# An attention and softplus-MLP kernel: the scheduler's order and pools replaced by one written list of steps and places, and GpSimd's copies and subtractions given to the other engines

## The chip, the cores and the metric

One NeuronCore of a Trainium2 chip. The metric is the device time of one execution in microseconds (us). TensorE is PE in the profile, VectorE DVE, ScalarE ACT, GpSimd POOL, and SyncE (which issues all DMAs here) SP.

## The reference

```python
B, H, S, Ns, D = 8, 8, 512, 32, 64          # x: (B, H, S, D), state: (B, H, Ns, D)
a      = softmax(x @ state^T / 8)           # over the 32 states
xread  = a @ state                          # (B, H, 512, 64)
a2     = softmax(state @ x^T / 8)           # over the 512 positions
sread  = a2 @ x                             # (B, H, 32, 64)
X = concat(xread, sread) -> (B * 544, 512)  # heads side by side
h = X @ w_in                                # 512 -> 2048
out = softplus(h) @ w_out                   # 2048 -> 512, (4352, 512) in float32
```

`w_in` and `w_out` arrive as float64 and are turned into float32 on the chip, by integer operations on their halves.

## The kernel before

**What is computed how.** The 512 rows `xread` of a batch are never formed. Since `xread @ w_in = a @ (state @ w_in)`, the kernel first forms V = state x w_in for every batch, and the hidden layer is then the attention weights times V. The 32 rows `sread` of each batch are formed and multiplied with w_in at the end for all batches together ("the read rows"). To keep float32's accuracy at the speed of fp32r, nearly every operand is split into a high part in fp32r (a copy that rounds) and a low part (the difference), and a product is three matmuls: high x high, high x low, low x high. A split is one copy and one subtraction of a 128x512 tile:

```python
def split(hi, lo, src, *what):
    if ("hi",) + what in MOVED:
        pool_copy(hi, src)                                  # GpSimd, L98
    else:
        nc.scalar.copy(hi, src)                             # ACT, L105
    vec(*what).tensor_tensor(lo, src, f32(hi), ALU.subtract)  # L106, DVE, or GpSimd where MOVED says so
```

Lines that matter in the profile:

- L112 loads a float64 tile. L129 or L136 (ACT; L134 on GpSimd) scales its high word, L131 (DVE, one instruction) or the pair L140, L141 (DVE, on 16-bit halves) shapes the low word, L142 (DVE) joins them.
- L185 and L194 (first chunk of 512 columns, two halves of 256), L227 and L238 (the other three chunks): plain float32 products of w_in with the state, for batches 0 and 1, and for 2 and 3. L190 to L199, L232 to L243 copy them out of PSUM. The converted weights and the products for batches 2 and 3 go out to DRAM.
- L262: the products for batches 4 to 7, by reading the weights back and splitting them (L276 or L98, L277) and copying the result out (L265, L267), in the stretch from about 200 us on.
- L322 loads x transposed, 512 KB at once. L369: scores of batches 0 and 1 in plain float32; L375: of the others in fp32r, whose two halves L379 and L380 add. L383 to L401: softmax over the states (transpose, maximum, difference, exponential, sum, product, transpose back); L406 to L415 over the positions. L425 transposes (TensorE), L443 and L449 read x, L455 to L469 scale, L477 and L486 transpose to `sreadT`.
- L513: the hidden layer of one of 16 tiles of 128 units ("h", six matmuls of 512 columns). L500: softplus. L520: the output layer, twelve matmuls of one tile for four chunks of 128 rows, into four accumulators "acc". L560: hidden layer of the read rows. L609 and L612: partial sums of batches 0 and 1. L160 and L162 copy the accumulators out, L528 stores them.

**What sets the order.** The program is written as strings of letters (START, BLOCK, LAST and others), each letter one piece of work: a hidden tile, an output tile, a split, a load, a step of the softmax. A scheduler then places the instructions on the engines' queues. The tile turns are: batch 0, tiles 0 to 3; batch 1, tiles 0 to 7; batch 0, 4 to 11; batch 1, 8 to 15; batch 0, 12 to 15; then batches 2 to 6, then the read rows, then batch 7. The weights of w_in and w_out are converted along the way. Buffers come from pools by tags with one to four buffers each; of PSUM's eight banks two belong to "aux" (scores, products, transposes), two to h and four to acc. The set MOVED names copies and subtractions that go to GpSimd.

Of the kernel before, what the change touches and what calls it, by code (L numbers as in the profile page):

```python
# [49 lines left out]
def attention_then_softplus_mlp(ctx: ExitStack, tc, xn, xt, zq, zp, stk, w_in, w_out, out):  # L50
    nc = tc.nc
    nc.scalar.preload_act_table_set("natural_log_exp_and_others")

    cp = ctx.enter_context(tc.tile_pool(name="cp", bufs=1))
    sp = ctx.enter_context(tc.tile_pool(name="sp", bufs=1))
    dp = ctx.enter_context(tc.tile_pool(name="dp", bufs=1, space=DRAM))
    ps = ctx.enter_context(tc.tile_pool(name="ps", bufs=1, space=PSUM))
    uid = [0]

    def sb(tag, shape, dt=F32, bufs=1):  # L60
        uid[0] += 1
        return sp.tile(shape, dt, tag=tag, name=f"{tag}_{uid[0]}", bufs=bufs)

    def bank(tag, bufs):
        uid[0] += 1
        return ps.tile([P, 512], F32, tag=tag, name=f"{tag}_{uid[0]}", bufs=bufs)

    BANKS = {"aux": 2, "h": 2, "acc": 4}
    turn = cycle(("h", "acc", "acc"))
    early = [True]  # L70

    def aux():
        if early[0]:
            tag = next(turn)
            return bank(tag, BANKS[tag])
        return bank("aux", 2)

    ident = cp.tile([P, P], F32, name="ident")
    make_identity(nc, ident)


    if WARM:
        idle = sb("sr", [P, P], bufs=2)
        nc.vector.memset(idle, 0.0)
        pb = aux()
        for _ in range(WARM):
            nc.tensor.matmul(pb[:, 0:P], idle, idle, start=True, stop=True)

    def rouse():
        pb = aux()  # L90
        for c in range(4):
            nc.tensor.transpose(pb[:, P * c:P * c + P], ident, ident)

    def vec(*what):
        return nc.gpsimd if what in MOVED else nc.vector

    def pool_copy(dst, src):
        nc.gpsimd.tensor_scalar(dst, src, 1.0, 0.0, ALU.mult, ALU.add)  # L98


    def split(hi, lo, src, *what):
        if ("hi",) + what in MOVED:
            pool_copy(hi, src)
        else:
            nc.scalar.copy(hi, src)  # L105
        vec(*what).tensor_tensor(lo, src, f32(hi), ALU.subtract)  # L106

    def load_w(src, tag=None):
        w64 = src.dtype == I64
        tag = tag or ("k4" if w64 else "wt")  # L110
        t = sb(tag, src.shape, I64 if w64 else F32, bufs=K4 if tag == "k4" else 2)
        nc.sync.dma_start(t, src)  # L112
        return t

    def as_f32(t, *what, tag="wt"):  # L120
        if t.dtype != I64:
            return t
        v = t.bitcast(I32).rearrange("p (n t) -> p n t", t=2)
        lo, hi = v[:, :, 0], v[:, :, 1]
        n = t.shape[1]
        h2 = sb("k2", [P, n], bufs=K2)
        r = sb(tag, [P, n], bufs=2 if tag == "wt" else 1)
        if early[0] or ("pre",) + what in MOVED:
            nc.scalar.activation(h2, f32(hi), AF.Prelu, scale=2.0 ** -112, alpha=-(2.0 ** 32))  # L129
            u = r.bitcast(I32)  # L130
            nc.vector.tensor_scalar(u, lo, 29, None, ALU.logical_shift_right)  # L131
        else:
            if ("h2",) + what in MOVED:
                nc.gpsimd.tensor_scalar(h2, f32(hi), 2.0 ** -112, 0.0, ALU.mult, ALU.add)  # L134
            else:
# [205 lines left out]

# [404 lines left out]
```

## Time and profile before

| | us |
|---|---|
| runs | 695.63, 697.95, 699.69 (median 697.95) |
| the profiled execution, first to last instruction | 695.4 |
| first float64 tile's conversion starts on DVE | 7.67 |
| TensorE, busy | 675.9 in 3028 matmuls |
| DVE, ACT, POOL, busy | 395.0, 390.9, 218.4 |
| moved by DMA | 82.90 MB |

The profiled execution has no other time of its own than its span, which lies at the lower end of the runs. A matmul's busy time in the profile overlaps that of the next one, so TensorE's share says that it has work nearly always and not how fast it goes through it; the starts of a string of matmuls tell that. Start times are counted from the span's start.

### The profile page before, as it was taken

How to read it: one execution, taken by the hardware profiler on the slowest of the kernel's cores; microseconds unless marked ns; L12 is line 12 of the kernel's file. 1: busy time of each engine (PE TensorE's matmuls, PEld its weight loads, DVE VectorE, ACT ScalarE, POOL GpSimd, SP SyncE). 2: the span in 40 equal slices, each digit the busy share in tenths (PEclk: the TensorE clock that was granted, in tenths of full speed). 3: DMA queues.
4: the chain of work that ended last, by engine and by line, in shares of the span. 5: the costliest groups of instructions: out<-in, count | busy, mean ns of one | idle time of the engine just before them, and what ended most of it. 6: DMA issues, size and time to landing. Idle time of an engine off the chain costs nothing.

```text
span 695.4 us, 8922 instructions
## 1 busy us (share of the span) xinstructions
PE 675.9 (97%) x3028; PEld 540.1 (78%) x3028; DVE 395.0 (57%) x692; ACT 390.9 (56%) x661; POOL 218.4 (31%) x209
## 2 busy tenths in 40 slices
PE   7879999999999999999999999999999999999997
PEld 4456667788887877888888888888888889988886
DVE  5898788319777885776556752676257423311101
ACT  4787975434848944775538634863386334423321
POOL 0130157146433584156222450235022400121310
PEclk9999999999999999999999999999999999999999
DMA  7778895103253545464423220321121113512001
GB/s 253 258 258 293 307 301 188 49 0 122 68 167 122 184 156 166 143 199 136 134 94 121 69 90 31 107 76 31 31 69 45 40 39 98 168 30 61 1 0 61
DMA packets 42061, 82.90 MB, mean 119 GB/s; under 512 B 6176, under 2 KB 13088, under 8 KB 42016
## 3 DMA queue, kind: packets, MB, share of 16 engines
q1 hardware_dynamic: 42016, 82.33, 36.1%
q8 instruction: 24, 0.39, 0.2%
q14 instruction: 21, 0.17, 0.1%
HBM read 56.62 MB, written 25.69 MB: 118 GB/s over the span
## 4 chain that ended last, share of the span: by engine, by line
PE 83%; ACT 7%; DVE 5%; DMA 2%; issue 1%; POOL 1%; SPq 0%; POOLq 0%; DVEq 0%; ACTq 0%
PE acc L520 49%; PE h L513 22%; PE h L560 3%; PE aux L262 2%; PE aux L449 2%; PE aux L375 1%; ACT L500 1%; DMA xT<-in_xt_dram 1%; ACT t L500 1%; PE aux L425 1%; PE aux L238 1%; PE aux L227 1%; DMA k<-in_w_in_dram 1%; ACT ghi L105 1%; DVE glo L106 1%
## 5 line engine op out<-in xcount | busy, mean ns | idle before, releaser
L520 PE MATMUL acc<-wout,ghi 128*128 128x512 f32 x1088 | 341.7, 395 | 3.9 <-POOL wout L98 2.8
L520 PEld LDWEIGHTS acc<-wout,ghi 128*128 128x128 f32 x1088 | 203.8, 189 | 50.7 <-issue 3.6
L520 PE MATMUL acc<-wout,glo 128*128 128x512 f32 x544 | 214.2, 394 | 0.0
L513 PE MATMUL h<-aT,vhl 128*128 128x512 f32 x768 | 199.4, 398 | 0.1
L513 PEld LDWEIGHTS h<-aT,vhl 128*128 128x128 f32 x768 | 142.1, 188 | 35.3 <-issue 3.4
L500 ACT ACTIVATE t<-h 128x512 f32<-128x512 f32 x136 | 81.0, 598 | 121.4 <-PE h L513 81.1
L106 DVE TENSOR_TENSOR glo<-t,ghi 128x512 fp32r<-128x512 f32 x83 | 63.7, 770 | 124.2 <-ACT ghi L105 83.9
L106 POOL TENSOR_TENSOR glo<-t,ghi 128x512 fp32r<-128x512 f32 x53 | 70.9, 1338 | 159.5 <-ACT ghi L105 156.7
L520 PEld LDWEIGHTS acc<-wout,glo 128*128 128x128 f32 x544 | 102.4, 188 | 23.0 <-issue 0.7
L105 ACT CAST ghi<-t 128x512 fp32r<-128x512 f32 x96 | 59.1, 618 | 76.1 <-PE acc L520 75.6
L106 DVE TENSOR_TENSOR vhl<-vf,vhl 128x512 fp32r<-128x512 f32 x57 | 41.5, 728 | 58.6 <-ACT vhl L105 48.4
L98 POOL TENSOR_SCALAR ghi<-t 128x512 fp32r<-128x512 f32 x40 | 28.7, 718 | 82.1 <-PE acc L520 39.5
L105 ACT CAST vhl<-vf 128x512 fp32r<-128x512 f32 x60 | 37.1, 618 | 17.3 <-PE h L513 11.3
L500 ACT ACT_TABLE_LOAD x23 | 29.5, 1283 | 7.8 <-DVE glo L106 5.7
L380 DVE TENSOR_TENSOR sc<-aux,k 64x512 f32<-64x512 f32 x24 | 16.4, 683 | 23.4 <-ACT k L379 23.1
L98 POOL TENSOR_SCALAR vhl<-vf 128x512 fp32r<-128x512 f32 x12 | 8.4, 696 | 66.8 <-PE h L513 50.7
L277 DVE TENSOR_TENSOR R<-wt,R 64x512 fp32r<-64x512 f32 x23 | 18.8, 819 | 10.4 <-ACT R L276 7.3
L560 PEld LDWEIGHTS h<-sreadT,vhl 128*128 128x128 f32 x192 | 24.1, 191 | 0.6
L560 PE MATMUL h<-sreadT,vhl 128*128 128x256 f32 x192 | 24.3, 283 | 0.0
L106 POOL TENSOR_TENSOR vhl<-vf,vhl 128x512 fp32r<-128x512 f32 x15 | 21.9, 1457 | 6.4 <-ACT vhl L105 6.0
L262 PE MATMUL aux<-R,StK 128*128 128x512 f32 x64 | 19.1, 398 | 1.2 <-POOL R L277 0.7
L398 POOL TENSOR_TENSOR T<-T,mx 128x512 f32<-128x512 f32 x7 | 7.7, 1106 | 37.3 <-DVE mx L397 17.4
(156 smaller groups left out, 736.3 us busy)
## 6 DMA issues: line engine op xcount, KB each, us to landing
vd<-ve SPq DMA_DIRECT2D x44, 256.0 KB, 2.7
xT<-in_xt_dram SPq DMA_DIRECT2D x16, 512.0 KB, 3.7
k<-in_w_out_dram SPq DMA_DIRECT2D x16, 512.0 KB, 5.1
x<-in_xn_dram SPq DMA_DIRECT2D x16, 512.0 KB, 3.5
vf<-vd SPq DMA_DIRECT2D x64, 128.0 KB, 2.6
k<-in_w_in_dram SPq DMA_DIRECT2D x12, 512.0 KB, 4.9
out_dram<-o SPq DMA_DIRECT2D x24, 256.0 KB, 2.2
vf<-vd SPq DMA_DIRECT2D x16, 256.0 KB, 4.0
```

What stands on the lines that cost most here:

```text
L98: nc.gpsimd.tensor_scalar(dst, src, 1.0, 0.0, ALU.mult, ALU.add)
L105: nc.scalar.copy(hi, src)
L106: vec(*what).tensor_tensor(lo, src, f32(hi), ALU.subtract)
L262: nc.tensor.matmul(pb, StK[i][:, h, :], r, start=(i == 0), stop=(i == 1))
L277: vec("R", *what, o).tensor_tensor(r[z], wf[a], f32(r[a]), ALU.subtract)
L380: nc.vector.tensor_tensor(sc[64 * j:64 * j + 64], pb[0:64], s2, ALU.add)
L398: vec("tmul", bk, g).tensor_tensor(T, T, sm.unsqueeze(2).broadcast_to([P, 16, NS]), ALU.mult)
L449: nc.tensor.matmul(pb[:, 256 * j:256 * j + 256], a2T[:, c, j].rearrange("p i n -> p (i n)"), v["xs"][j][:, c].rearrange("p i n -> p (i n)" ...
L500: nc.scalar.activation(t, h, AF.Softplus)
L513: nc.tensor.matmul(h, Vhl[b, ft // 2][:, vi, g, cs], aT[b][:, ai, g], start=(n == 0), stop=(n == 5))
L520: nc.tensor.matmul(acc[c], g[gi][:, c0:c0 + P], wout[ft][:, wi], start=(ft == first and i == 0), stop=(ft == last and i == 2))
L560: nc.tensor.matmul(h[:, 256 * i:256 * i + 256], Whl[u, i][:, wi, kt, :], sreadT[:, si, kt, :], start=(n == 0), stop=(n == 11))
```

## The change

The scheduler, the strings and MOVED go. The kernel first describes all its work as a graph of 2598 named steps with their inputs and outputs, and then walks a list, PLAN, that names each step in order, the engine that does it, and the place of every buffer that it makes: one of 69 single or 14 double places in SBUF, or one of PSUM's eight banks, which any kind of buffer may have.

```diff
-START = 'avaavaaavaavaavavavaavaaaaBpbW|bvbbbbboVbvbbbWV|bbbbVVWVaVVbVaaaaaaabbbVbap|bbbaiWgVgpVboVob|iVpbViW|gbWV|biVVibgbog|pVigW|bbVp|VoWVgi|VogpVb|ViVVpVg|
...
+PLAN = """
+Lq.1:S:0 Li.0.3:S:1 Lz.0:S:2 zn.0:G:3 Lt.0.0.0:S:4 Lt.0.0.1:S:5 Li.0.2:S:6 Li.0.7:S:7 Li.0.0:S:8 Lt.0.1.0:S:9 Lq.0:S:10 Lo.1:S:0 ch.0.3:A:11
...
+    with tc.manual_schedule():
...
+        ops = graph(io, at, nc)
+        for step in PLAN.split():
+            name, e, where = step.split(":")
+            step = ops.pop(name)
+            where = [int(w) for w in where.split(",") if w]
+            for buf in step.places():
+                if buf not in place:
+                    put(buf, where.pop(0))
+            step.emit(e)
```

The engine letters are A and C for ACT (two forms of the high half), V and W for DVE (W is the low half in two instructions), T for TensorE, S for SP, and G for GpSimd. The products, their splits and the order in which each accumulator adds up are those of before. What else is different:

- GpSimd does two clearings of a tile and the identity matrix at the start, and nothing later: its instructions go from 215 to 14. DVE's go from 695 to 784 (subtractions and the like of 128x512 from 224 to 320), ACT's from 648 to 751 (copies of 128x512 from 208 to 276; table loads from 46 to 36). TensorE's matmuls stay at 3028.
- x transposed is loaded in halves of 256 KB, and V is fetched for 256 columns at a time, so that SP issues 421 DMAs for about 325, with the same bytes.

Three places show how instructions move. In the rows the numbers behind a name are the buffer's.

The first is SP's queue at the program's start, where `xT` is x transposed, `Z`, `zf` and `QZ` the state in two layouts, `k` and `w` float64 tiles of w_in, `o` of w_out, and `x` x itself; before:

```order
L322 DMA xT_102<-in_xt_dram 128x1024
L334 DMA Z_84<-in_zp_dram 128x2x64 x2
L112 DMA k_6_104<-in_w_in_dram 128x256
L112 DMA k_7_106<-in_w_in_dram 128x256
L322 DMA xT_108<-in_xt_dram 128x1024
L112 DMA k_9_110<-in_w_in_dram 128x256
```

and now:

```order
L292 DMA QZ_103<-in_zq_dram 128x512
L292 DMA w_0_3_105<-in_w_in_dram 128x256
L292 DMA zf_107<-in_zp_dram 128x256
L292 DMA xT_0_0_111<-in_xt_dram 128x512
L292 DMA xT_0_1_113<-in_xt_dram 128x512
L292 DMA w_0_2_115<-in_w_in_dram 128x256
L292 DMA w_0_7_117<-in_w_in_dram 128x256
```

The first float64 tile has moved from the fourth of the queue's issues to the second, and x transposed from the first to the fourth, in two pieces.

The second is DVE ahead of the output layer of batch 1's tiles 4 and 5, where `glo`, now `gL`, are the low parts of the softplus, `wt`, `wf` and `ow` converted weights; before:

```order
L142 SCALAR_TENSOR_TENSOR wt_843<-k_240_842,wt_843 128x512
L140 TENSOR_SCALAR k_252_874<-k_248_868 128x512
L141 TENSOR_SCALAR k_252_874<-k_248_868 128x512
L142 SCALAR_TENSOR_TENSOR wt_872<-k_250_871,k_252_874 128x512
L106 TENSOR_TENSOR glo_790<-t_787,ghi_789 128x512
L140 TENSOR_SCALAR k_262_915<-k_217_747 128x512
L106 TENSOR_TENSOR wout_249_870<-wt_872,wout_249_870 128x512
L141 TENSOR_SCALAR k_262_915<-k_217_747 128x512
```

and now:

```order
L336 TENSOR_SCALAR ow_902<-o_10_576 128x512
L337 TENSOR_SCALAR ow_902<-o_10_576 128x512
L482 TENSOR_SCALAR rs<-rs 128x1
L483 RECIPROCAL rs<-rs 128x1
L341 SCALAR_TENSOR_TENSOR ow_902<-h_o_724,ow_902 128x512
L482 TENSOR_SCALAR rs<-rs 128x1
L483 RECIPROCAL rs<-rs 128x1
L301 TENSOR_TENSOR gL_4_928<-t_4_905,gH_4_915 128x512
L301 TENSOR_TENSOR gL_5_932<-t_5_907,gH_5_924 128x512
L527 TENSOR_SCALAR sr_939<-rp_0_735,rs 128x2x2x64
```

Both low parts of the softplus now stand on DVE, one behind the other, where DVE had one of them among the conversions and their splits and the next could go to GpSimd.

The third is TensorE at the first products for batches 4 to 7 (`aux`, now `pp`; `R` are split weights, `StK`, now `KH` and `KL`, the split state); before:

```order
L520 MATMUL acc_2124<-wout_128_451,ghi_1967 128x512
L262 MATMUL aux_2032<-R_1981,StK_1896 128x512
L262 MATMUL aux_2041<-R_1982,StK_1896 128x512
L520 MATMUL acc_2124<-wout_128_451,ghi_1967 128x512
L262 MATMUL aux_2032<-R_1981,StK_1896 128x512
L262 MATMUL aux_2041<-R_1982,StK_1896 128x512
L520 MATMUL acc_2124<-wout_128_451,glo_1968 128x512
```

and now:

```order
L304 MATMUL acc_0_2_2032<-Wl_1059,gH_9_2304 128x512
L304 MATMUL acc_0_2_2032<-Wh_1048,gL_9_2314 128x512
L304 MATMUL pp_0_0_2334<-R_0_2276,KH_0_2007 128x512
L304 MATMUL pp_0_0_2334<-R_0_2276,KL_0_2254 128x512
L304 MATMUL pp_0_4_2338<-R_4_2297,KH_1_2190 128x512
L304 MATMUL pp_0_4_2338<-R_4_2297,KL_1_2202 128x512
L304 MATMUL pp_0_1_2343<-R_1_2316,KH_0_2007 128x512
L304 MATMUL pp_0_1_2343<-R_1_2316,KL_0_2254 128x512
L304 MATMUL acc_0_1_2090<-Wh_1048,gH_9_2304 128x512
```

Two products that were woven into the output layer through the two banks of "aux" have become three, whole and one after the other, in banks 6, 7 and 4 of the eight.

More of the change, by code (lines that the diff above doesn't have):

```diff
@@ L1 @@
 from contextlib import ExitStack
-from itertools import cycle
 import concourse.bass as bass
@@ new lines, in width, with rounded @@
+def width(buf):
+    kind, *at = buf.split(".")
+    whole = at and at[0] in map(str, range(WHOLE))
+    if kind in ("vp", "pp", "qp", "gp", "rp", "tp", "h", "acc") or kind == "sc" and whole:
+        return 0
+    if kind in ("o8", "x", "xs", "Wf", "Vk"):
+        return 2
+    return 2 if kind == "w8" and at[0] != "0" or kind == "aa" and not whole else 1
+def rounded(buf):
+    kind, *at = buf.split(".")
+    return kind in ("KH", "KL", "R", "Vh", "Vl", "aH", "aL", "xh", "xl", "xs", "Wh", "Wl", "gH", "gL", "uH", "uL") \
+        or kind in ("z", "aa") and int(at[0]) >= WHOLE
@@ L89, in rouse @@
[L89 to L106, printed above, removed]
@@ L492, in split_wout @@
-    def split_wout(ft):
-        assert ft < NFT - 1 or all(made[0, c] == 3 for c in range(1, 4))
-        wout[ft] = sb(f"wout{ft}", [P, 2, DM], F32R)
-        w = as_f32(ahead("out"), ft)
-        split(wout[ft][:, 0], wout[ft][:, 1], w, "wout", ft)
-    def softplus(h, *what):
-        t = sb("t", [P, 512], bufs=2)
-        nc.scalar.activation(t, h, AF.Softplus)
-        ghi = sb("ghi", [P, 512], F32R, bufs=3)
-        glo = sb("glo", [P, 512], F32R, bufs=3)
-        split(ghi, glo, t, "g", *what)
-        return ghi, glo
@@ L506, in gemm1 @@
-    def gemm1(b, ft):
-        h = bank("h", 2)
-        n = 0
-        cs = slice(P * (ft % 2), P * (ft % 2) + P)
-        assert made["aT", b] == 2
-        for g in range(2):
-            for vi, ai in PASSES:
-                nc.tensor.matmul(h, Vhl[b, ft // 2][:, vi, g, cs], aT[b][:, ai, g], start=(n == 0), stop=(n == 5))
-                n += 1
-        return softplus(h, min(b, 4), ft)
-    def gemm2(acc, g, ft, cols, first=0, last=NFT - 1):
-        for c, c0 in enumerate(cols):
-            for i, (gi, wi) in enumerate(PASSES):
-                nc.tensor.matmul(acc[c], g[gi][:, c0:c0 + P], wout[ft][:, wi],
-                                 start=(ft == first and i == 0), stop=(ft == last and i == 2))
@@ L553, in gemm1_read @@
-    def gemm1_read(u):
-        assert made["read"] == B
-        h = bank("h", 2)
-        for i in range(2):
-            n = 0
-            for kt in range(4):
-                for wi, si in PASSES:
-                    nc.tensor.matmul(h[:, 256 * i:256 * i + 256], Whl[u, i][:, wi, kt, :], sreadT[:, si, kt, :],
-                                     start=(n == 0), stop=(n == 11))
-                    n += 1
-        return softplus(h, B, u)
-    COLS = [0, P, 2 * P, 3 * P]
-    QTR = NFT // 4
@@ L686, in attention_then_softplus_mlp @@
-    run(START)
-    assert made["read"] == 3
-    for b in range(2, B - 1):
-        run({2: BLOCK2, 3: BLOCK3}.get(b, BLOCK), b)
-    run("|gFp" * (NFT // 2))
-    run(LAST)
-    while pend:
-        flush(True)
+    io = IO()
+    io.xn, io.xt, io.zq, io.zp, io.stk, io.w_in, io.w_out, io.out = xn, xt, zq, zp, stk, w_in, w_out, out
+    io.wsc = [dp.tile([DM, 512], F32, tag=f"wsc{c}", name=f"wsc{c}") for c in range(4)]
+    io.Vd = {}
+    for c in range(4):
+        io.Vd[0, c] = dp.tile([H, P, 512] if c in PACKED else [P, 4, 512], F32, tag=f"vd0_{c}", name=f"vd0_{c}")
+        io.Vd[1, c] = dp.tile([H, P, 512], F32, tag=f"vd1_{c}", name=f"vd1_{c}")
@@ new lines, in attention_then_softplus_mlp, with put @@
+    ident = cp.tile([P, P], F32, name="ident")
+    sreadT = cp.tile([P, 2, 4, B * NS], F32R, name="sreadT")
+    fixed = {"ident": ident, "sreadT": sreadT.bitcast(F32)}
+    for n, w in SMALL.items():
+        t = cp.tile([P, 2 * B, w], F32, name=n)
+        for b in range(B):
+            for g in range(2):
+                fixed[f"{n}.{b}.{g}"] = t[:, 2 * b + g, :]
+    place = {}
+    def put(buf, i):
+        n = width(buf)
+        if n == 0:
+            place[buf] = ps.tile([P, 512], F32, tag=f"bank{i}", name=buf.replace(".", "_"), bufs=1)
+        else:
+            t = sp.tile([P, 512 * n], F32R if rounded(buf) else F32, tag=f"{'sd'[n - 1]}{i}", name=buf.replace(".", "_"), bufs=1)
+            place[buf] = t.bitcast(F32) if rounded(buf) else t
@@ new lines, in at @@
+    def at(buf):
+        return fixed[buf] if buf in fixed else place[buf]
+    with tc.manual_schedule():
+        make_identity(nc, ident)
+        put("idle", 0)
+        put("h.idle", 0)
+        nc.vector.memset(at("idle")[:, 0:P], 0.0)
+        for _ in range(WARM):
+            nc.tensor.matmul(at("h.idle")[:, 0:P], at("idle")[:, 0:P], at("idle")[:, 0:P], start=True, stop=True)
+        ops = graph(io, at, nc)
[6 more added lines that the diff above has]
+                    put(buf, where.pop(0))
+            assert not where
+            step.emit(e)
+        assert not ops
```

1081 lines of the change are left out of this document (585 added, 496 removed).

## The prediction

> **What bounds the kernel now.** I read the page first, then the chain of work that ended last, then the engines by stretches, then TensorE's groups and waits in the first stretch. The lines are the page's busy times, the end of the chain, and five stretches (length, then busy time and count for PE, PEld, DVE, ACT, POOL, then granted clock, DMA share, GB/s).
>
> ```profile
> PE 675.9 (97%) x3028; PEld 540.1 (78%) x3028; DVE 395.0 (57%) x692; ACT 390.9 (56%) x661; POOL 218.4 (31%) x209
> ...
> 675.29 16.33 PE acc L520 x72
> ...
> 0.00:90.70 90.70, 77.83 (x283) 51.56 (x284) 70.00 (x158) 69.77 (x131) 16.23 (x20) 0.98 0.79 275
> 90.70:200.00 109.30, 108.18 (x467) 85.41 (x466) 73.45 (x114) 62.42 (x102) 46.66 (x46) 1.00 0.37 120
> 200.00:300.00 100.00, 98.40 (x436) 78.43 (x436) 75.07 (x124) 64.92 (x109) 45.95 (x44) 1.00 0.50 159
> 300.00:691.20 391.20, 391.06 (x1846) 324.71 (x1845) 176.04 (x299) 193.17 (x321) 109.55 (x100) 1.00 0.23 71
> 691.20:695.40 4.20, 0.41 (x2) 0.00 (x0) 0.46 (x1) 0.58 (x1) 0.00 (x0) 1.00 0.66 247
> ```
>
> TensorE sets the end, but its 97% hides the only place with room. A record's busy time overlaps the next one's, so I count by spacing: 16.33/72 = 0.2268 us for a 512-column product in fp32r. From 300 to 691.2 TensorE runs without a gap, and the change leaves its 1846 matmuls there as they are: nothing to gain. In the first 90.7 us it starts only 283. Their groups (count, busy, mean ns, idle ahead), two strings that give the spacing in plain fp32, and its two largest waits:
>
> ```profile
> L520 PE MATMUL acc<-wout,ghi 128*128 128x512 f32 x50 | 18.4, 448 | 3.8 <-POOL wout L98 2.8 <-ACT wout L105 1.0
> L513 PE MATMUL h<-aT,vhl 128*128 128x512 f32 x60 | 17.8, 427 | 0.0
> L520 PE MATMUL acc<-wout,glo 128*128 128x512 f32 x25 | 11.5, 458 | 0.0
> L369 PE MATMUL aux<-xT,Z 128*128 128x512 f32 x16 | 8.9, 683 | 3.8 <-DMA xT<-in_xt_dram 3.6 <-DMA Z<-in_zp_dram 0.2
> L443 PE MATMUL aux<-x,a2T 128*128 128x256 f32 x32 | 7.4, 383 | 0.0
> L238 PE MATMUL aux<-wt,wout 128*128 128x512 f32 x10 | 5.3, 613 | 0.1
> ...
> L185 PE MATMUL acc<-wout,QZ 128*128 128x256 f32 x8 | 2.5, 388 | 1.2 <-DMA QZ<-in_zq_dram 1.2
> ...
> 25.86 1.98 PE L369 MATMUL aux<-xT,Z 128*128 128x512 f32 x4
> ...
> 53.81 3.48 PE aux L443 x16
> ...
> PE aux L369 <- DMA xT<-in_xt_dram: 3.6, 2, 1.9
> PE acc L520 <- POOL wout L98: 2.8, 1, 2.8
> ```
>
> Plain fp32 of 512 columns is spaced (1.98 - 0.683)/3 = 0.43, of 256 columns 3.48/16 = 0.2175. So the 283 are worth 135 x 0.2268 = 30.6 (L520, L513), 16 x 0.43 = 6.9 (L369), 28 x 0.43 = 12.0 (four groups of L227 and L238, one shown), 64 x 0.2175 = 13.9 (L443, and L185 with L194, one of seven groups shown) and 24 transposes at about a quarter of 0.43, 2.6; the rest are the warm-up, worth nothing. That is 66 us of work in 90.7: **24.7 us are lost there**, of the 41 that the span holds over all its matmuls at these spacings. DVE and ACT are occupied 70.00 and 69.77 of these 90.7 us, and their product is what TensorE waits for. The change is decided here; all else is small.
>
> **The change part by part.** First the prices: DVE's and POOL's subtraction (83 and 53 of them), ACT's and POOL's copy, a table load; then DVE's low halves of a float64 weight in two instructions (15 pairs, L140 and L141) and in one (L131), and a subtraction under POOL's.
>
> ```profile
> L106 DVE TENSOR_TENSOR glo<-t,ghi 128x512 fp32r<-128x512 f32 x83 | 63.7, 770 | 124.2 <-ACT ghi L105 83.9
> L106 POOL TENSOR_TENSOR glo<-t,ghi 128x512 fp32r<-128x512 f32 x53 | 70.9, 1338 | 159.5 <-ACT ghi L105 156.7
> ...
> L105 ACT CAST ghi<-t 128x512 fp32r<-128x512 f32 x96 | 59.1, 618 | 76.1 <-PE acc L520 75.6
> ...
> L98 POOL TENSOR_SCALAR ghi<-t 128x512 fp32r<-128x512 f32 x40 | 28.7, 718 | 82.1 <-PE acc L520 39.5
> ...
> L500 ACT ACT_TABLE_LOAD x5 | 6.4, 1283 | 0.1
> ...
> L140 DVE TENSOR_SCALAR k<-k 128x512 uint16<-128x512 uint16 x15 | 7.3, 490 | 1.0 <-DMA k<-in_w_in_dram 1.0
> L141 DVE TENSOR_SCALAR k<-k 128x512 uint16<-128x512 uint16 x15 | 7.2, 480 | 0.0
> L106 DVE TENSOR_TENSOR glo<-t,ghi 128x512 fp32r<-128x512 f32 x6 | 4.1, 686 | 0.3 <-ACT ghi L105 0.3
> L131 DVE TENSOR_SCALAR wt<-k 128x512 int32<-128x512 int32 x4 | 1.7, 423 | 1.8 <-DMA k<-in_w_out_dram 1.8
> ...
> 24.27 1.05 POOL L398 TENSOR_TENSOR T<-T,mx 128x512 f32<-128x512 f32 x1
> ...
> 24.39 1.49 DVE L106 TENSOR_TENSOR vhl<-vf,vhl 128x512 fp32r<-128x512 f32 x1
> ```
>
> A subtraction on DVE takes 0.69 alone and 1.49 while POOL subtracts. So POOL's subtractions gave DVE little: 1.34 of POOL's time, of which DVE pays up to 0.8.
>
> *DVE up to the same TensorE work (the first product of tile 5 of the second batch, matmul 283).* By its new order 31 large subtractions stand ahead, against 22 on DVE and 4 on POOL before: 9 more for DVE, +6.2. Two max-subtractions or products of the softmax come from POOL: +1.4. Low halves of 512 columns: 7 pairs and 11 single ones against 15 pairs and 4, -8 x 0.97 + 7 x 0.42 = -4.8; two of 256 columns become pairs, +0.5; one joining of halves more, +0.7. Some four evacuations at 256 or 512 columns fewer: -1.4. No slowed instructions: -1.7. Seven small subtractions of the read rows (0.22 each) come later: -1.5. Sum: -0.6, so DVE has **69.4 us to do, as before**. ACT: ten more casts, five of them POOL's, +6.2; one high half more, +0.7; three table loads fewer, -3.8; seven small casts later, -1.4; three evacuations and a scaling fewer, -2: **-0.3, 69.5 us**. POOL's 16 us are absorbed. The engines' work therefore gives no speed by itself; what may is that they idle less than 90.7 - 70 = 20.7 us.
>
> *When they start.* The first row is the first float64 load, the fourth of the old queue's issues; the second DVE's first conversion, which waited for it.
>
> ```profile
> 1.43 1.32 SPq L334 DMA_DIRECT2D Z<-in_zp_dram  x2
> 2.79 1.08 SPq L112 DMA_DIRECT2D k<-in_w_in_dram  x2
> ...
> 7.67 0.29 DVE L131 TENSOR_SCALAR wout<-k 128x256 int32<-128x256 int32 x1 [6.67 <-DMA k<-in_w_in_dram]
> ```
>
> It took 7.67 - 2.79 = 4.9 from issue to use. Now it is issued second, where the state's load was issued at 1.43: 6.3, a gain of 1.4. If all idling after that stays (90.7 - 7.67 - 70 = 13.0), matmul 283 starts at 6.3 + 69.4 + 13.0 = **88.7: the upper end**.
>
> *The lower end* is set by the DMA queue. In the new order 10.1 MB stand on it up to the weight tile with which the second chunk of columns begins on DVE (its low half), and 25.8 us of DVE's 69.4 ahead of that. At the first stretch's 275 GB/s it lands at 36.7, so at least 11 us of DVE's idling stay, and matmul 283 can't start before 36.7 + 69.4 - 25.8 + one subtraction (0.7) = **81**. Between 81 and 88.7 I take two thirds toward the upper, 86.2, since the waits that make it up (ACT's high half, transfers of w_out) are between instructions that the new order still sets close. The gain here is 90.7 - 86.2 = **4.5 us**. Two reads of the first batch now stand ahead of TensorE's first h product, and their x tiles behind some 7.9 MB, so about 29 us: covered by the 20 us that TensorE has to spare by then, but not if DVE ran ahead.
>
> *From 90.7 on.* In 200 to 300 the five largest groups hold 409 fp32r products:
>
> ```profile
> L520 PE MATMUL acc<-wout,ghi 128*128 128x512 f32 x154 | 48.4, 392 | 0.2 <-DVE StK L612 0.2
> L513 PE MATMUL h<-aT,vhl 128*128 128x512 f32 x123 | 31.5, 392 | 0.0
> L520 PE MATMUL acc<-wout,glo 128*128 128x512 f32 x78 | 30.5, 391 | 0.0
> L262 PE MATMUL aux<-R,StK 128*128 128x512 f32 x38 | 11.6, 402 | 1.2 <-POOL R L277 0.7 <-DVE sreadT L106 0.6
> L375 PE MATMUL aux<-k,zhl 128*128 128x512 f32 x16 | 4.7, 397 | 0.1
> ...
> PE aux L227 <- DVE wout L232: 1.1, 1, 1.1
> ```
>
> 92.8 us and some 3 of smaller ones: 4 lost. Of that 1.2, with 1.1 behind L232 at 97, are waits for POOL and for copies that DVE did late: **2.3 gained** if the written order has them earlier, and 0 if others come in their place. DVE gets POOL's 21 subtractions of this stretch (75.07 + 21 x 0.69 = 89.6 of 100) and ACT its 23 copies (64.92 + 23 x 0.62 = 79): covered by TensorE's 100, thinly for DVE. After 300 both have over 190 us idle, so the rest of POOL's 109.55 costs nothing. More and smaller DMAs (421 against about 325): 96 issues at about 0.54 (1.08 for two, above), 52 us on a queue that only issues; after the first 90 us nothing waits for it. The tail of 4.20 (the last products' copies and stores) keeps its form.
>
> Sum: 695.4 - 4.5 - 2.3 = 688.6 of span. The median of the runs, 697.95, stands 2.55 above the profiled span (the runs are 695.63 to 699.69, the span about the lowest): **691**.
>
> For the copies there is a rule that speaks against their move. Row: POOL's copy 718 ns, ACT's 618, and POOL's subtraction 1338 against 770. The Trainium skill, "GPSIMD Engine Reference", section 4.1, says that one-input operations run there at about line rate and only two-input ones at about half of VectorE's; the rows agree. By that rule moving the copies only loads ACT, by 7 x 0.62 = 4.3 us in the first 90 (five copies and two high halves); had ACT nothing to set against it, the time would be 695.5.
>
> **The rivals.** *No change, 697.* DVE and ACT idle as much as before (88.7, a gain of 2.0), and 90 to 300 keeps its waits: 693.4 + 2.55 = 696, and 697 with a wait of 1 us in a new place. For it: their occupied time is the same to 2 us, and a strict order stalls the whole engine at each late input.
>
> *Slower, 705.* Eight PSUM banks are now handed from buffer to buffer at once, where the score products and the packed products had two of their own. After 90 us 32 products (L262) and 24 pairs of scores (L375) each take a bank that an evacuation must have left. In 200 to 300 27 such places lost some 4 us, 0.15 each. If each of the 56 loses half an evacuation (0.3, by the copy's 0.62 above), 56 x 0.3 = 17 stand in the place of the 2.8 that the forecast leaves of them: 691 + 14 = **705**; it decides from 0.24 a place (13.2 in all, past 701.4). For it: in the written order up to three products of this kind stand back to back, and DVE is at 90% there. Against: the chain of needs, summed from the durations, leaves DVE and ACT 15 to 30 us ahead of TensorE from about 130 us on.
>
> *The clock, one step either way.* The row is five products after a gap, and the clock in the stretch behind it.
>
> ```profile
> 37.65 2.45 PE L520 MATMUL acc<-wout,ghi 128*128 128x512 f32 x5 [2.76 <-POOL wout L98]
> ...
> 38.00:39.00 1.00, 1.00 (x3) 0.76 (x3) 1.00 (x4) 1.00 (x3) 0.00 (x0) 0.50 0.31 115
> ```
>
> Half clock for about 3.4 us costs 1.7. TensorE was behind its inputs there anyhow, so it matters only past 60 us: at most 2 us, inside the range.
>
> **How the numbers follow.** A measurement of this kernel tells 0.5% (3.5 us) from no change at best: the same is 694.5 to 701.4. The forecast (faster) 0.45, no change 0.28, slower 0.27 (bank waits 0.2, other stalls 0.07). The forecast's own range is 686 (matmul 283 at 81, -9.7, and -2.3) to 694.5; for 8 in 10 the range takes in no change and most of the slower case: 685 to 705.
>
> **What would show it.** Right: matmul 283 at 81 to 89, DVE's busy time up to it near 69, no subtraction on DVE over 0.8, first conversion near 6.3; from 300 on the same distances. Wrong: waits of TensorE for an evacuation (L262's, L375's places) adding to over 5 us after 90; or DVE and ACT behind each other before 90, so that matmul 283 starts after 91; or the float64 tiles landing later than 275 GB/s gives.

## The result, and the profile after

The changed kernel takes 686.68 us (median of four runs, 686.29 to 687.10) against 697.39 before (695.63 to 699.69): ratio 0.9849, 95% interval 0.9823 to 0.9874. It is 10.7 us faster; the forecast was 691 with 685 to 705. The profiled execution took 686.29 with a span of 684.5. It moves 83.44 MB by DMA against 82.90 before, so the bytes are nearly, and not exactly, the same.

The changed kernel's page, its busy times; then the stretches (same columns as before the change), the first one ending where TensorE has done as much work as before at 90.7:

```profile
PE 668.1 (98%) x3028; PEld 541.5 (79%) x3028; DVE 403.8 (59%) x781; ACT 431.3 (63%) x764; POOL 1.6 (0%) x8
...
0.00:85.00 85.00, 74.73 (x286) 53.72 (x287) 69.53 (x154) 68.64 (x134) 1.63 (x8) 0.94 0.76 275
85.00:200.00 115.00, 115.00 (x491) 90.27 (x490) 73.88 (x138) 76.17 (x127) 0.00 (x0) 1.00 0.33 105
200.00:300.00 100.00, 97.55 (x436) 78.61 (x435) 68.29 (x120) 77.00 (x132) 0.00 (x0) 1.00 0.53 168
300.00:680.00 380.00, 379.99 (x1818) 318.59 (x1817) 192.07 (x372) 208.22 (x371) 0.00 (x0) 1.00 0.25 79
680.00:684.50 4.50, 0.81 (x4) 0.34 (x2) 0.00 (x0) 1.24 (x3) 0.00 (x0) 0.88 0.62 233
```

The first stretch holds the larger part of the gain: DVE and ACT are occupied for 69.53 and 68.64 us, as before the change (70.00, 69.77), POOL for 1.63 instead of 16.23, and the stretch is 5.7 us shorter. The two engines' work is the same and they idle less. How the engines begin, from their timelines (start, duration, idle ahead in brackets):

```profile
1.05 3.51 PE L764 MATMUL h_idle<-idle 128*128 128x128 f32 x16 [1.05 <-DVE idle L762]
...
4.59 0.39 SPq L292 DMA_DIRECT2D QZ<-in_zq_dram  x1
5.03 0.42 SPq L292 DMA_DIRECT2D w<-in_w_in_dram  x1
...
8.25 0.29 DVE L333 TENSOR_SCALAR wf<-w 128x256 int32<-128x256 int32 x1 [7.26 <-DMA w<-in_w_in_dram]
...
9.25 0.76 PE L304 MATMUL vp<-wf,QZ 128*128 128x256 f32 x1 [4.69 <-DVE wf L341]
```

And TensorE's largest waits over the whole run (sum, times, longest; `vp` is a product for V, `gp` a transpose of the exponentials `e`, `sc` the scores of the first two batches, `pp` the products for batches 4 to 7):

```profile
PE vp L304 <- DVE wf L341: 4.7, 1, 4.7
PE gp L490 <- ACT e L479: 2.4, 1, 2.4
PE sc L304 <- DMA xT<-in_xt_dram: 1.6, 1, 1.6
PE pp L304 <- DVE R L362: 1.2, 1, 1.2
PE acc L304 <- DVE gL L301: 1.1, 2, 1.0
```

The reader is to see two things. No wait is on POOL any more. And the first DMA is issued at 4.59, where it was 0.74 before: TensorE's longest wait, 4.7 us, stands behind it, and so does every other load.

Where the time went is clearest from what TensorE has lost by a given amount of work, counted by the prediction's spacings (start of the matmul that stands there, less the work ahead of it), in us. The columns on the right belong to the experiments.

| work done | before | changed | warm-up tile moved | before, no GpSimd | changed, GpSimd back | copies back | subtractions back |
|---|---|---|---|---|---|---|---|
| 15 | 13.8 | 17.3 | 12.6 | 16.9 | 17.9 | 16.8 | 18.2 |
| 66 | 24.9 | 19.0 | 14.4 | 25.2 | 22.6 | 19.5 | 21.2 |
| 180 | 27.7 | 19.6 | 15.0 | 27.3 | 25.9 | 20.2 | 22.5 |
| 300 | 32.5 | 24.6 | 20.2 | 30.1 | 34.7 | 27.5 | 29.7 |
| 650 | 36.8 | 26.0 | 21.7 | 34.4 | 36.2 | 28.9 | 31.1 |

Of the 10.8 us won, 5.9 come by 66 us of work, 2.2 up to 180, nothing between 180 and 300 (4.8 lost before, 5.0 now), 2.9 after 300 (4.3 lost before, 1.4 now).

### The profile page after: what moved, and what is told of

Read it like the earlier page. It is cut to its first block, busy times and chain, and to the rows that moved or that the text cites. A ratio compares the mean times of both kernels' runs of the same rounds, so it can differ in the third digit from the quotient of the medians.

```text
span 684.5 us, 8918 instructions
## 1 busy us (share of the span) xinstructions
PE 668.1 (98%) x3028; PEld 541.5 (79%) x3028; DVE 403.8 (59%) x781; ACT 431.3 (63%) x764; POOL 1.6 (0%) x8
## 2 busy tenths in 40 slices
DMA packets 51278, 83.44 MB, mean 122 GB/s; under 512 B 6688, under 2 KB 26144, under 8 KB 51232
## 3 DMA queue, kind: packets, MB, share of 16 engines
q1 hardware_dynamic: 51232, 82.86, 36.8%
## 4 chain that ended last, share of the span: by engine, by line
PE 85%; ACT 6%; DVE 5%; DMA 2%; issue 1%; SPq 0%; DVEq 0%; ACTq 0%
PE acc L304 49%; PE h L304 25%; PE vp L304 2%; PE rp L304 2%; PE pp L304 2%; PE qp L304 2%; DMA out_dram<-o 1%; DMA xT<-in_xt_dram 1%; PE gp L490 1%; ACT Vk L285 1%; ACT t L633 1%; PE sc L304 1%; PE h_idle L764 1%; DVE Vl L301 0%; DVE wf L341 0%
## 5 line engine op out<-in xcount | busy, mean ns | idle before, releaser
L304 PE MATMUL acc<-Wh,gH 128*128 128x512 f32 x544 | 216.7, 398 | 0.0
L304 PE MATMUL acc<-Wh,gL 128*128 128x512 f32 x544 | 212.1, 390 | 1.1 <-DVE gL L301 1.1
L304 PE MATMUL acc<-Wl,gH 128*128 128x512 f32 x544 | 212.0, 390 | 0.0
L301 DVE TENSOR_TENSOR gL<-t,gH 128x512 fp32r<-128x512 f32 x136 | 92.3, 687 | 168.5 <-ACT gH L285 163.7
L304 PEld LDWEIGHTS acc<-Wh,gL 128*128 128x128 f32 x544 | 102.1, 188 | 23.7 <-DVE gL L301 2.1
L304 PEld LDWEIGHTS acc<-Wl,gH 128*128 128x128 f32 x544 | 102.2, 188 | 22.4 <-issue 2.2
L304 PEld LDWEIGHTS acc<-Wh,gH 128*128 128x128 f32 x544 | 102.2, 188 | 22.4 <-issue 2.2
L304 PE MATMUL h<-aH,Vh 128*128 128x512 f32 x256 | 102.7, 401 | 0.5 <-ACT o L285 0.2
L304 PE MATMUL h<-aH,Vl 128*128 128x512 f32 x256 | 99.8, 390 | 0.0
L304 PE MATMUL h<-aL,Vh 128*128 128x512 f32 x256 | 99.7, 390 | 0.0
L304 PEld LDWEIGHTS h<-aL,Vh 128*128 128x128 f32 x256 | 48.1, 188 | 10.4 <-issue 1.0
L285 ACT CAST Vh<-Vf 128x512 fp32r<-128x512 f32 x48 | 29.7, 621 | 5.2 <-DMA Vf<-vd 5.2
L573 DVE TENSOR_TENSOR sc<-qp,qs 64x512 f32<-64x512 f32 x24 | 16.4, 683 | 14.9 <-ACT qs L571 14.4
```

The costliest lines, as they stand in the source:

```text
L285: nc.scalar.copy(dst, src)
L301: lambda e: eng(e).tensor_tensor(r(dlo()), src(), dhi(), ALU.subtract))
L304: nc.tensor.matmul(dst, lhs, rhs, start=start, stop=stop)
L573: lambda e, kj=kj, sc=sc, j=j: nc.vector.tensor_tensor(at(sc)[64 * j:64 * j + 64], at(f"qp.{kj}")[0:64], at(f"qs.{kj}")[0:64], ALU.add))
```

## The experiments

**The warm-up tile moved.** The row of the warm-up matmuls ends at 1.05 + 3.51 = 4.56, and the first DMA is issued at 4.59. Both have to do with place 0 of SBUF: the tile that the warm-up reads and the first load's target.

```diff
-        put("idle", 0)
+        put("idle", 68)
```

> The changed kernel, with one place moved: the tile that the eight warm-up matmuls read lies in another place of SBUF than the first load's target. In the changed kernel SP issues its first DMA at 4.59 us, just when the last warm-up matmul starts (4.46 to 4.56), where the kernel before issued at 0.74. Theory A (that load waits for the warm-up matmuls to have read their tile, and every other load stands behind it): first issue near 0.8, the first weight conversion 3.8 us earlier than 8.25, and the span shorter by 3 to 4.5 us: 682 to 684 us against 686.7, since TensorE loses 17.3 of its 26 us in the first 32. Rival B (the start is bound by how fast all the loads land, and TensorE by the work of VectorE and ScalarE, so an earlier first load is waited out later): first issue earlier but the span shorter by less than 1.5 us, over 685.

682.33 us (681.98 to 682.39), 4.35 under the changed kernel. Theory A holds. The timeline of this run:

```profile
0.73 0.39 SPq L292 DMA_DIRECT2D QZ<-in_zq_dram  x1
1.19 0.42 SPq L292 DMA_DIRECT2D w<-in_w_in_dram  x1
...
4.27 0.29 DVE L333 TENSOR_SCALAR wf<-w 128x256 int32<-128x256 int32 x1 [3.28 <-DMA w<-in_w_in_dram]
...
5.27 0.88 PE L304 MATMUL vp<-wf,QZ 128*128 128x256 f32 x2 [0.44 <-PE h_idle L764]
```

The first loads are issued 3.84 to 3.86 us earlier, and TensorE's loss at 66 us of work falls by 4.6, of which 4.3 are left at the end (26.0 to 21.7). The 0.5 beyond 3.86 is no larger than the spread of the runs, but the traces show the clock as a part of it. In the changed kernel TensorE stands idle from 4.56 to 9.25, and it has half its clock until about 17.8 (0.55 as the mean of 16 to 18 us). The changed kernel's stretches, and two strings of its matmuls:

```profile
6.00:8.00 2.00, 0.00 (x0) 0.00 (x0) 0.00 (x0) 0.00 (x0) 0.00 (x0) 0.89 0.88 297
8.00:10.00 2.00, 0.75 (x2) 0.50 (x2) 0.72 (x2) 0.43 (x1) 0.00 (x0) 0.50 0.73 157
16.00:18.00 2.00, 2.00 (x7) 1.43 (x5) 2.00 (x6) 0.74 (x2) 0.00 (x0) 0.55 1.04 388
...
15.60 3.89 PE L304 MATMUL vp<-wf,QZ 128*128 128x256 f32 x12
19.32 1.88 PE L304 MATMUL sc<-xT,z 128*128 128x512 f32 x4
```

With the tile moved, half the clock comes too, by the means of the stretches from about 9.1 to 12.5 us. These stretches, and TensorE's matmuls ahead of and in them:

```profile
8.00:10.00 2.00, 0.91 (x1) 0.47 (x2) 0.29 (x1) 0.34 (x1) 0.00 (x0) 0.78 1.02 387
10.00:12.00 2.00, 1.76 (x4) 0.56 (x3) 1.76 (x5) 0.97 (x3) 0.00 (x0) 0.50 1.04 413
12.00:14.00 2.00, 2.00 (x9) 1.61 (x8) 1.97 (x7) 1.11 (x3) 0.00 (x0) 0.87 1.05 393
...
6.79 1.10 PE L304 MATMUL sc<-xT,z 128*128 128x512 f32 x2 [0.64 <-DMA xT<-in_xt_dram]
9.09 2.02 PE L304 MATMUL sc<-xT,z 128*128 128x512 f32 x2 [1.20 <-DMA xT<-in_xt_dram]
11.35 3.49 PE L304 MATMUL vp<-wf,QZ 128*128 128x256 f32 x12 [0.24 <-DVE wf L341]
14.68 1.88 PE L304 MATMUL sc<-xT,z 128*128 128x512 f32 x4
```

The twelve products take 14.68 - 11.35 = 3.33 us here and 19.32 - 15.60 = 3.72 in the changed kernel, so 0.4 us goes with the shorter time at half clock. The Trainium skill, "TensorE: Matmul & The Clock Gate", Part 1, says that an idle window of about 3.4 us is enough for half the clock; the changed kernel's trace agrees with its 4.7 us gap. The run with the tile moved shows that less is enough: from 5.27 us on no gap of TensorE ahead of the half clock is longer than 1.20 us, and the gap ahead of it in the prediction is 2.76 us.

**GpSimd's work taken away, and nothing else.** The kernel before, with its own order:

```diff
     def vec(*what):
-        return nc.gpsimd if what in MOVED else nc.vector
+        return nc.vector
     def pool_copy(dst, src):
-        nc.gpsimd.tensor_scalar(dst, src, 1.0, 0.0, ALU.mult, ALU.add)
+        nc.scalar.copy(dst, src)
```

and the high halves of L134 on ACT in the same way.

> The kernel before, with its scheduler, strings and pools, and with every copy, subtraction and high half that GpSimd did done by ScalarE or VectorE. Theory A (the gain comes from the written order; the removal of GpSimd alone is worth little, since VectorE and ScalarE take over as much work as they win): 694 to 702 us, within 0.5% of 697.4. Rival C (GpSimd's subtractions slowed VectorE and that is what the change took away): 688 to 692 us, most of the gain, with matmul 283 before 88 us.

695.13 us (693.39 to 696.33), ratio to before 0.9972 (0.9957 to 0.9987): 1.7 us won (0.9 to 3.0), inside theory A's range. Its first stretch:

```profile
0.00:91.00 91.00, 77.71 (x283) 50.80 (x284) 70.98 (x162) 70.98 (x134) 1.17 (x7) 0.98 0.84 277
```

and its largest DVE group:

```profile
L106 DVE TENSOR_TENSOR glo<-t,ghi 128x512 fp32r<-128x512 f32 x136 | 93.5, 690 | 150.9 <-ACT ghi L105 102.0 <-ACT ghi L98 45.6 <-PE aux L262 2.0
```

The subtraction falls from 770 to 690 ns, and DVE takes over POOL's share for it: 70.98 us occupied against 70.00, and matmul 283 stands where it stood. The little that is won lies between 180 and 300 us of work (27.3 to 30.1, before 27.7 to 32.5).

**GpSimd's work put back into the written order.** The 201 pieces that GpSimd had, in the changed kernel's order and places; each edit is one letter:

```diff
- ... Nm.0.0:V: vh.0.0:A:46 ...
+ ... Nm.0.0:G: vh.0.0:A:46 ...
```

> The changed kernel's written order and places, with the same 201 copies, subtractions and high halves on GpSimd as before the change. Theory A (the order makes the gain): GpSimd's slower pieces come a little late at some places, 686 to 691 us. Rival C (leaving GpSimd out makes the gain): 694 us or more. The spacing of TensorE's matmuls after 300 us tells where the 1.3 ns a matmul come from that the change also won there: 228.6 again by C, 227.1 by A.

697.09 us (695.01 to 698.91), ratio to before 0.9992 (0.9975 to 1.0009): the whole gain is gone. Theory A, that the order makes the gain, fell with this. Its subtractions, by group:

```profile
L301 DVE TENSOR_TENSOR gL<-t,gH 128x512 fp32r<-128x512 f32 x83 | 67.7, 825 | 128.8 <-ACT gH L285 69.5 <-POOL gH L287 59.2
...
L301 POOL TENSOR_TENSOR gL<-t,gH 128x512 fp32r<-128x512 f32 x53 | 74.1, 1398 | 178.2 <-ACT gH L285 131.8 <-DMA Vf<-vd 11.9 <-issue 11.0
```

and TensorE's waits:

```profile
PE vp L304 <- DVE wf L341: 5.2, 3, 4.7
PE acc L304 <- POOL gL L301: 2.7, 3, 2.1
PE acc L304 <- DVE gL L301: 2.6, 2, 1.5
...
PE pp L304 <- POOL R L362: 1.8, 2, 1.0
```

DVE's subtractions take 825 ns, where they took 770 in the kernel before, and these rows have five waits of TensorE for POOL. By the table the loss comes early (22.6 against 19.0 at 66) and between 66 and 300 (12.1 against 5.6). Rival C doesn't hold either, since taking GpSimd out of the old order gave 1.7. So neither part alone gives the gain: it comes where this written order meets pieces as short as it counts on. Two things are not shown. An order written for GpSimd's pieces was not tried. And this run has the late first load too (a wait of 4.7 us), which costs the changed kernel 4.35; with the warm-up tile moved the order might keep some of its gain beside GpSimd. No run has both. After 300 us the order alone does it: matmuls of 512 columns there are spaced by a mean of 228.6 ns before and without GpSimd in the old order, and by 227.1 to 227.2 in the changed kernel and here (spacings above 0.3 us left out).

**The pieces by kind.** The same letters for the 92 pieces with one input alone, and for the 109 with two inputs alone.

> The changed kernel's order and places, with only the 92 operations of one input (copies and three high halves) on GpSimd as before the change; all subtractions stay on VectorE. With all 201 back the time was 697.1, ten above the changed kernel. Theory E (the written order has no slack for GpSimd's subtractions, 1.34 us against 0.69, and VectorE is slowed while they run; a copy takes 0.72 there against 0.62): 686 to 689 us. Rival F (any work on a third queue comes late in this order, whatever its kind): about half of the ten, 690 to 693.

> The changed kernel's order and places, with only the 109 operations of two inputs (subtractions, and the softmax's differences and products) on GpSimd as before the change; the copies stay on ScalarE. Theory E: nearly all of the ten us, 693 to 697, most of it before 90 us and between 200 and 310 us. Rival F: 690 to 693, as the copies alone.

Copies back: 689.12 us (688.17 to 689.49), 2.4 over the changed kernel. Subtractions back: 691.76 (689.53 to 693.93), 5.1 over it. Both together cost 10.4, so 2.9 appear only with both back (2.2 by the table at 650). With runs that spread over 4.4 us this size is rough, and why it appears isn't told apart. Theory E has the order of the two right and the copies just past its upper end, but asked for more from the subtractions than they cost; rival F has the number of the subtractions and not that of the copies. Neither is the whole. The subtraction in the changed kernel, then groups of the run with the copies, then of that with the subtractions:

```profile
L301 DVE TENSOR_TENSOR gL<-t,gH 128x512 fp32r<-128x512 f32 x136 | 92.3, 687 | 168.5 <-ACT gH L285 163.7
```

```profile
L301 DVE TENSOR_TENSOR gL<-t,gH 128x512 fp32r<-128x512 f32 x136 | 96.9, 720 | 161.4 <-ACT gH L285 111.8 <-POOL gH L287 44.4 <-DMA out_dram<-o 4.4
...
L287 POOL TENSOR_SCALAR gH<-t 128x512 fp32r<-128x512 f32 x40 | 29.8, 748 | 291.5 <-ACT t L633 260.6 <-DVE xl L301 16.6 <-ACT gH L285 8.0
```

```profile
L301 DVE TENSOR_TENSOR Vl<-Vf,Vh 128x512 fp32r<-128x512 f32 x36 | 34.4, 961 | 26.6 <-ACT Vh L285 21.8 <-DMA Vf<-vd 4.8
...
L301 POOL TENSOR_TENSOR gL<-t,gH 128x512 fp32r<-128x512 f32 x53 | 72.9, 1376 | 296.1 <-ACT gH L285 230.5 <-issue 17.9 <-DMA Vf<-vd 11.9
```

Even copies on POOL stretch DVE's subtraction, from 687 to 720 ns; subtractions on POOL stretch one group of DVE's to a mean of 961. The Trainium skill, "GPSIMD Engine Reference", section 1, says that GpSimd shares its ways into SBUF with VectorE and contends with VectorE's instructions of two SBUF inputs; both runs agree.

**Where the buffers lie.** The single places of SBUF renumbered at random, place 0 kept; the same buffers still follow each other:

```diff
+    mp = {0: 0, **dict(zip(range(1, 69), shuffled))}     # every place of one width in PLAN
```

> The changed kernel with its single places in SBUF renumbered at random (place 0 stays, so the first load waits as before). Order, engines and which buffers share a place are the same. After 300 us TensorE's matmuls of 512 columns are spaced 227.1 ns in the changed kernel and 228.6 before, with GpSimd or without. Theory G (the order of the matmuls makes this): 227.1 again, and 686.7 us within 0.7. Rival H (where the buffers lie makes it): another spacing, 228 or more, and 2 us or more on the time.

687.54 us (685.52 to 689.13) and a spacing of 227.1 ns: the spacing is not made by the places, and rival H fell. The time is 0.9 over the changed kernel, just past theory G's 0.7, and its spread covers that. What in the order makes the 1.4 ns was not varied by itself; what the traces show of it stands under "After 300" below.

**One place handed on too early.** Beside the moved warm-up tile:

```diff
- s.2.2:A:56
+ s.2.2:A:12
```

> As the first of these, and the softplus output of batch 2's tile 2 lies in a place that matmuls leave free (12) and not in one that a store of a partial sum still reads (56). In the changed kernel ScalarE waited 2.27 us for that store there, and TensorE 1.1 us for the low part behind it, and 0.3 again for the next. Theory A (a place handed on too early): ScalarE's wait for the store goes, TensorE's wait at 206 shrinks from 1.4 to under 0.4, and the time is 1 us under that of the first. Rival D (the next late input takes its place): no difference to the first, within 0.4 us.

682.01 us (681.30 to 682.26), 0.3 under the run with the warm-up tile alone, as rival D says. The row without the edit, and the row that took its place with it:

```profile
201.55 0.60 ACT L633 ACTIVATE t<-h 128x512 f32<-128x512 f32 x1 [2.71 <-DMA out_dram<-o]
```

```profile
202.01 0.69 DVE L301 TENSOR_TENSOR gL<-t,gH 128x512 fp32r<-128x512 f32 x1 [3.80 <-DMA out_dram<-o]
```

ACT's wait for a store is gone, and the next buffer in the chain, the low part on DVE, waits for the next store. TensorE's wait for that low part goes from 1.4 to 1.0 us only, where theory A had under 0.4. Four partial sums are stored together there and their places are all reused at once.

**The start, four runs further.** All with the warm-up tile moved, and the later ones on top of the first. First, one exponential earlier on ACT:

```diff
- E.0.1:V: V1.0.6:T:2 ch.0.4:A:47 vl.0.0:V:48 Q.1.1:T:7 kh.0.1:A:49 cu.0.4:V:50
- Sw.0.6:S: ve.0.6:A:51 N.0.1:V: e.0.1:A:52 Li.1.2:S:9
+ E.0.1:V: e.0.1:A:52 V1.0.6:T:2 ch.0.4:A:47 vl.0.0:V:48 Q.1.1:T:7 kh.0.1:A:49 cu.0.4:V:50
+ Sw.0.6:S: ve.0.6:A:51 N.0.1:V: Li.1.2:S:9
```

> The kernel with the warm-up tile moved (682.3 us), and the exponential over the positions of batch 0's second pair of heads ahead of two ScalarE steps that it stood behind. TensorE waited 2.5 us for it at 22 to 24 us, the longest wait left. Theory I (TensorE's start is bound by single late inputs): that wait shrinks to about 1.3 and the time falls by 0.5 to 1.2. Rival J (VectorE is without a gap from 10 to 25 us and bounds the start, so the next product then waits for a converted weight instead): the same wait under another name and no difference, within 0.4.

681.79 us (680.34 to 683.01). The wait shrank as theory I said, and a wait of 0.4 for a converted weight followed, as J said; 0.5 us is less than the spread. It is the lowest median of all kernels here, not told apart from the one with the warm-up tile alone: ratio to before 0.9783 for both.

```profile
PE gp L490 <- ACT e L479: 1.4, 1, 1.4
```

Then the first tile of w_out loaded and converted later, with nothing else changed from the last run:

```diff
- ... Lo.1:S:0 ch.0.3:A:11 ... ch.o1:A:36 ... cu.o1:V:37 ... cr.o1:V: ... wh.1:A:41 ...
+ ... ch.0.3:A:11 ... Lo.1:S:0 Lo.2:S:2 ... ch.o1:A:36 cu.o1:V:37 cr.o1:V: wh.1:A:41 ch.o0:A:68
```

> The kernel of the last run (681.8 us), with the first tile of w_out loaded (512 KB) and converted on ScalarE and VectorE some 15 us later, just before the other tiles of w_out, instead of between the first weights of w_in. Theory K (the first 25 us are bound by the bytes and by VectorE's work that stand ahead of the softmax and the first weights, and some slack is left behind): the weights behind it land up to 1.3 us earlier, VectorE saves 1.1 us there, and the time falls by 1 to 2 us, to 680. Rival L (VectorE and ScalarE have no slack up to 85 us either, so the work moved is missing later): no difference, within 0.5 us.

684.02 us (683.31 to 684.97), 2.2 worse. This speaks for rival L and beyond it: TensorE's loss goes up by 2 us between 20 and 25 us of work, where it waits for ACT's softplus behind the pieces that were moved.

```profile
PE h L304 <- ACT t L633: 1.2, 1, 1.2
```

ACT and DVE have no room there. Last, the second tile of w_in ahead of x transposed, with w_out's tile late and with it where it was:

```diff
- Li.0.3:S:1 Lz.0:S:2 zn.0:G:3 Lt.0.0.0:S:4 Lt.0.0.1:S:5 Li.0.2:S:6
+ Li.0.3:S:1 Li.0.2:S:6 Lz.0:S:2 zn.0:G:3 Lt.0.0.0:S:4 Lt.0.0.1:S:5
```

> The same, and the second tile of w_in is loaded ahead of the state and x transposed for the first scores, not behind them. VectorE is idle for 3.4 us from 5.8 to 9.2, waiting for that tile. Theory K: the wait shrinks by 1 to 1.5 us, and the scores come up to 0.7 us later, so another 0.5 us, 679.5. Rival L: VectorE's order puts the next steps behind the scores, which come later, so no gain or 0.5 us lost.

> The 681.8 us kernel (warm-up tile moved, one exponential earlier; w_out's first tile where it was), with only the second tile of w_in loaded ahead of the state and x transposed. With w_out's tile late this load order took 1.1 us off (684.0 to 682.9), too little to tell from the spread. Theory M (VectorE bounds the start, and its 3.4 us of waiting for that tile are worth filling): lag of TensorE at 5 us of work 8.6 against 9.5, and 680.5 to 681.3 us. Rival L: the scores come later by as much, 681.5 to 682.5.

682.94 us (681.69 to 686.10) and 682.25 (681.47 to 686.52): no gain that can be told. In the second, the scores wait 2.8 us for x transposed instead of 1.4, as rival L says.

```profile
PE sc L304 <- DMA xT<-in_xt_dram: 2.8, 1, 2.8
```

## Why the prediction was right, point by point

- *The engines' work up to matmul 283.* Forecast 69.4 us for DVE and 69.5 for ACT; measured 69.53 and 68.64. That this gives nothing by itself was right: the same work without GpSimd in the old order (70.98 each) left matmul 283 where it was.
- *When they start.* This step was wrong. Forecast 6.3 us, measured 8.25. It took the first load to be issued as early as before, and didn't see that the load's target is the place from which the warm-up matmuls read. That cost 3.86 us at the queue and 4.35 in the end, as the run with the other place shows. The other part of the term was off too: from issue to use it took over the old queue's 4.9 us, and in that run it is 4.27 - 1.19 = 3.1, so without the shared place DVE would have started two microseconds ahead of the forecast.
- *The idling after the start.* The term that was mis-sized, to the other side. Forecast 13.0 us at the upper end, 10.5 at the value taken; measured 85.0 - 8.25 - 69.53 = 7.2. By luck the two errors nearly cancel: matmul 283's place in the work is reached at 85.0 for a forecast of 86.2, 4.5 us of gain for a measured 5.9 at equal work. With the warm-up tile moved it is at 80.4; of the four runs that changed the start further three gave nothing that can be told, and one lost 2.2.
- *The lower end.* 80.4 is close to its 81, but not for its reason. The tile of the second chunk was to land at 36.7 and to hold DVE up. DVE takes that tile with no wait ahead of the step, at 40.66 in the changed kernel and at 36.04 with the warm-up tile moved:

```profile
40.66 0.42 DVE L333 TENSOR_SCALAR wf<-w 128x512 int32<-128x512 int32 x1
...
36.04 0.42 DVE L333 TENSOR_SCALAR wf<-w 128x512 int32<-128x512 int32 x1
```

- *From 90.7 to 300.* Forecast 2.3, measured 2.2, all of it up to 180 us of work, where 1.1 was expected: the sum agrees by luck. The 1.2 expected between 200 and 300 didn't come: waits for POOL gave way to waits for low parts and split weights on DVE (1.1 and 1.2), behind reused places and ACT's queue.
- *After 300.* "Nothing to gain" failed: 2.9 us. The loss there was taken as TensorE's own; it is mostly a spacing of 228.6 ns that the new order brings to 227.1. One period of the order, the 322 matmuls that it repeats for each batch, takes 71.2 us before (442.2 to 513.4), with GpSimd's work and without it, and 70.4 after (452.5 to 522.9). The old order has five strings of short matmuls (up to 256 columns) in it and the new one three, and of the 296 matmuls of 512 columns 83 to 88 are spaced above 229 ns in the old one and 13 to 19 in the new. Most of these stand behind the short strings, and most of the others go at 226 to 227 ns in both. That the number of strings makes the difference is read from these traces; no run changed it alone. Two strings of the chain as examples, before (24 matmuls, 230 ns each) and after (33, 227 ns each):

```profile
555.80 5.53 PE acc L520 x24
```

```profile
672.65 7.48 PE acc L304 x33
```

- *The run beside its span.* 2.55 us were added to the span; the median of the four runs stands 686.68 - 684.5 = 2.18 over the profiled one's. The whole miss of 4.5 us (691.15 before rounding) is then 1.4 up to matmul 283, 2.9 after 300 and 0.4 here, less 0.1 or so in between.
- *The rivals.* "No change" is what either half of the change gives alone, 695.1 and 697.1. The slower rival, bank waits at 56 places, had no ground: after 85 us TensorE's only waits above 0.3 us are the 1.2 for a split weight and the 1.1 for low parts, none for an evacuation. The half clock came, for some 10 us at the start of the changed kernel; 0.4 us of what it cost can be read off, inside the 2 us of the forecast.
- *The signs.* Matmul 283, DVE's busy time and the subtractions came as named (none on DVE over 0.70 us, where 0.8 was the limit). The first conversion near 6.3 and the same distances from 300 on did not.

## What to carry to other kernels

Count what each engine has to do up to the place where TensorE first runs free: if that doesn't change, only idling can be won there. Here a written order won it only together with the shorter pieces that it was written for. In a written list of places, look first at who else reads the place of the very first load: one shared tile cost 4.35 us here, four tenths of what the whole change brought. When work is moved off a full stretch, find where it lands before counting it as won.

## What the runs showed of the hardware that was not expected

- GpSimd's copies with one input slow DVE's subtractions too: 687 ns alone, 720 with 92 such pieces in the program, as a mean over all 136.
- Matmuls of 512 columns can keep a spacing above 229 ns behind a string of short ones, 33 to 36 of the 48 that follow one of these strings in the old order and at most nine behind any in the new one. The means over 300 to 680 us are 228.6 in the old order, with GpSimd's work and without it, and 227.1 to 227.2 in the new one, with it, without it, and with the single places mixed. What makes the recovery long or short stays open.
- TensorE's clock fell to half from about 9.1 to 12.5 us in the run with the warm-up tile moved, though no gap between its matmuls there was longer than 1.20 us.
